# A state-space block and a gated mixture on one core: products of the first chunk moved to GpSimd, second scores ahead of the first outputs, and a carried state moved within the fourth step

## The chip, the cores and the metric

One core of a Trainium2 chip runs the whole kernel. The metric is device time in microseconds of one execution; the kernel before has a median of 639.62 us over four runs (639.5 to 639.63). TensorE is called PE, VectorE DVE, ScalarE ACT, GpSimd POOL and SyncE SP, as in the profile.

## The reference, cut to what matters

Two blocks follow one another. The first is a recurrent block (4 sequences, 8 heads, 768 tokens, head size 32, state size 16), worked in chunks; the second sends its output, seen as 3072 tokens of width 256, through four experts and adds them with normalised weights.

```python
# first block, for each chunk
cum = np.cumsum(la, axis=-1)                       # la = log(clip(a))
L = np.exp(cum[..., :, None] - cum[..., None, :]) * causal
M = np.einsum('bhin,bhjn->bhij', Cc, Bc) * L       # scores, masked by decays
y = M @ xc + (Cc @ state) * exp(cum)
state = decay_full * state + sum over the chunk of B x decay_from_j
# second block
p = domain_probs / (domain_probs.sum(-1, keepdims=True) + 1e-09)
for e in range(E):                                 # E = 4, F = 1024
    out += p[:, e:e + 1] * (np.maximum(x @ w1[e], 0) @ w2[e])
```

## The kernel before, in words

**Chunks.** The first block is worked in 24 chunks of 128 tokens of one sequence, all eight heads at once. The first four (numbers 0 to 3) are the beginnings of the four sequences, the next four continue them, and so on. For a chunk c these helpers exist:

- `spread(c)` (L331, PE) copies the decays a of chunks 0 to 2 to all partitions, into four PSUM banks; later chunks get them by a DMA, `load_decays` (L134, tile ab), from a DRAM copy acut_d that `store_decays(0)` writes from ScalarE's queue (L286). `store_decays(1)` does the same for ac_d, which `load_heads` reads (L146, tile ah).
- `decay_part(c, 0)` and `decay_part(c, 1)` (L364, DVE) are scans that make the decay matrices LT of the two halves of the heads. Part 1 ends with a GpSimd product that writes the decayed B into the last columns of MT (L369). `decay_part(c, 2)` is for chunks with an incoming state: a scan dec of ah (L347, DVE) and its product with C, cts (L350, POOL).
- `masks(c)` (L378, ACT) writes ctm, the rows of C of the even and the odd heads apart. `scores` (L393, PE) makes the scores g in four PSUM tiles of two heads each, numbered 0 to 3.
- `masked(cs, rs)` (L405, DVE) multiplies scores by LT into MT, one instruction for each number. `aside(c, q)` does one number in another way: ScalarE copies g to SBUF (gs, L412) and GpSimd multiplies (L413).
- `outputs` (L462, PE) and, for chunk 1, `outputs_apart` (L428) make y from MT; ScalarE copies it to yT (L471, L432) and the chunk's own state to A (L478, L435).
- `carry(c)` (L486 to L493, DVE) turns A into the state that the next chunk of that sequence receives: a transpose S and a product M with a mask.

**Steps.** The second block is worked in six blocks of 512 tokens (128 of each sequence, four chunks), each in eight steps n (four experts, two halves of an expert's width). From step 2 on, the products are arranged in seven where eight would be plain (fmul, L523, for the first layer; smul, L608, for the second), on sums of the weights that GpSimd makes (L189 to L193) and stores for later blocks (L201, L207). In a step, `snap` copies a PSUM bank (ACT, L530), `total` adds it to the other bank (DVE, L535, tile z), `gated` applies the maximum and the expert's weight (DVE, L545, tile h) and `diff` makes differences of gated tiles (DVE, L552, tile hT). The two PSUM banks of the first layer are X and Y; the steps that make chunk 4 and later use X and Y for two of the four score tiles as well.

**What sets the order.** The order is written out by hand: each engine gets its instructions in the order in which the Python code records them, and semaphores hold an instruction until its data and its buffer are ready. The first chunks are a written list at the end of the function (from `turn(1)` on). Then a loop over n records each step, and chunks 4 and later are spread over it: `scanned` chunks get their LT, `scored` chunks their masks, scores and masked products, `done` chunks their outputs. Work left from the step before is in the list `late`: two differences and, behind them, a `carry`. In the steps of the first block that score chunks (n = 3 and n = 6, where `behind` is true), the first two entries of `late` come behind the first gated tile, and the carry and `decay_part(c, 2)` behind `gated(n, "21", "X")`, directly in front of the scores:

```python
        gated(n, "21", "X")
        for work in late[2:] if behind else []:
            work()
        for c in scored if behind else []:
            decay_part(c, 2)
```

The ScalarE copies of `aside` and of `outputs` stand in one queue, so the order of the calls decides which is first.

Of the kernel before, what the change touches and what calls it, by code (L numbers as in the profile page):

```python
# [17 lines left out]
def kernel(  # L18
# [68 lines left out]
    att = ctx.enter_context(tc.tile_pool(name="att", bufs=2))  # L87
    ffn = ctx.enter_context(tc.tile_pool(name="ffn", bufs=2))
    ps_att = ctx.enter_context(tc.tile_pool(name="ps_att", bufs=2, space=bass.MemoryType.PSUM))
    ps_f = ctx.enter_context(tc.tile_pool(name="ps_f", bufs=1, space=bass.MemoryType.PSUM))  # L90
    ps_s = ctx.enter_context(tc.tile_pool(name="ps_s", bufs=1, space=bass.MemoryType.PSUM))
# [15 lines left out]
    def turned_round(c):  # L107


        return c >= CPB and c % 2 == 1  # L110
# [44 lines left out]
    def load_w1(n):  # L155
        e, jj = divmod(n % SPB, JJ)
        t1 = wt1[n] = wts.tile([P, 7, HB], FP32, tag="wt1", name="wt1", bufs=5)
        for k in range(2):
            w = 2 - 2 * k
            a_ = 2 if n < SPB or k else 1  # L160
            nc.sync.dma_start(
                out=t1[:, w:w + a_],
                in_=w1[e, k * P:k * P + P].rearrange("p (a f) -> p a f", a=2)[
                    :, 0:a_, jj * HB:jj * HB + HB])
        if n >= SPB:
            nc.sync.dma_start(out=t1[:, S3:], in_=w1_d[n % SPB])
# [117 lines left out]
    def store_decays(kind):  # L284
        d, sb = ((acut_d, a_cut), (ac_d, a_sb))[kind]
        nc.scalar.dma_start(  # L286
            out=d.rearrange("c h s -> (c h) s").rearrange("(p r) s -> p r s", r=2), in_=sb)
# [3 lines left out]
    def turn_gates(pool, tag):  # L291

        rows = T // P * E
        pp = pool.tile([rows, P], FP32, tag=tag, name="pp")
        nc.tensor.transpose(pp, pr.rearrange("p i e -> p (i e)"), ident[:, 0])
        p_sb = const.tile([rows, P], FP32, name="p_sb")
        gate["rows"] = p_sb
        nc.scalar.copy(out=p_sb, in_=pp)
# [24 lines left out]
    def spread(c, homes):  # L323


        s = st[c]
        s["a"] = []
        for q, (pool, tag) in enumerate(homes):
            k = slice(32 * q, 32 * q + 32)
            b = pool.tile([P, NT * P], FP32, tag=tag, name="a")  # L330
            nc.tensor.matmul(  # L331
                out=b, lhsT=one[k].to_broadcast([32, P]), rhs=a_q[k, c].rearrange("p t s -> p (t s)"),
                start=True, stop=True, tile_position=(32 * q, 0))
            s["a"].append(b)

    def decays(c):
        for part in range(3):
            decay_part(c, part)
# [34 lines left out]
    def masks(c):  # L373

        s = st[c]
        m = s["ctm"] = att.tile([HN, NT, P], FP32, tag="ctm", name="ctm")
        for t in range(NT):
            nc.scalar.mul(m[:, t], s["xb"][:, OCT:OCT + P], tmask[:, t:t + 1])  # L378

    def scores(cs, homes):  # L380

        for c in cs:
            st[c]["g"] = {}
        for r, (pool, tag) in enumerate(homes):
            g = pool.tile([P, len(cs), NT, P], FP32, tag=tag, name="g")
            for j, c in enumerate(cs):
                st[c]["g"][r ^ 2 * turned_round(c)] = g[:, j]
        for j, c in enumerate(cs):
            s = st[c]
            for r in range(NQ):  # L390
                k = slice(32 * r, 32 * r + 32)
                g = s["g"][r ^ 2 * turned_round(c)]
                nc.tensor.matmul(  # L393
                    out=g.rearrange("p t s -> p (t s)"), lhsT=s["xb"][k, OBT:OBT + P],
                    rhs=s["ctm"][k].rearrange("p t s -> p (t s)"),
                    start=(j == 0), stop=True, tile_position=(32 * r, 0),
                    skip_group_check=True)

    def masked(cs, rs):
        for r in rs:  # L400
            for c in cs:
                q = r ^ 2 * turned_round(c)
                h = slice(NT * q, NT * q + NT)
                s = st[c]
                nc.vector.tensor_mul(s["MT"][:, h, 0:P], s["g"][q], s["LT"][:, h])  # L405

    def aside(c, q):

        s = st[c]
        h = slice(NT * q, NT * q + NT)  # L410
        g = att.tile([P, NT, P], FP32, tag="gs", name="gs")
        nc.scalar.copy(out=g, in_=s["g"][q])  # L412
        nc.gpsimd.tensor_mul(s["MT"][:, h, 0:P], g, s["LT"][:, h])  # L413
# [322 lines left out]
    turn(1, 3)  # L736
    masks(0)
    scores([0], homes)
    store_decays(0)
    decays(0)  # L740
    aside(0, 3)
    masks(1)
    load_w1(1)
    load_tokens(3)
    load_decays(3)
    load_w2(0)
    spread(1, banks)
    masked([0], (2, 0, 1))
    turn_gates(ps_att, "att")
    outputs([0])  # L750
    scores([1], ((ps_f, "X"), (ps_s, "acc0"), (ps_s, "acc1"), (ps_att, "att")))
    decay_part(1, 0)
    aside(1, 0)
    decay_part(1, 1)
# [61 lines left out]
    late = []  # L816
    states = [2, 3]
    for n in range(PLAIN, NS):
        k, r = divmod(n, SPB)

        ahead = CPB * (k + 1)
        scanned = [ahead + d for d in {0: [0], 2: [1], 4: [2], 5: [3]}.get(r, [])]
        scored = [ahead + d for d in {3: [0, 1], 6: [2, 3]}.get(r, [])]
        done = [ahead + d for d in {4: [0, 1], 7: [2, 3]}.get(r, [])]
        if k == NBLK - 1:
            scanned, scored, done = [], [], []
        ending = r == 0 and k > 0
        e = r // JJ
        if r % JJ == 0 and n + JJ < NS:
            load_gate(*divmod(n // JJ + 1, E))  # L830
        if PLAIN + 2 < n + 2 < NS:
            load_w1(n + 2)
            load_w2(n + 2)
        opened(n)
        total(n, 1, "11")
        gated(n, "11", "z11")
        behind = scored and k == 0
        for work in late[:2] if behind else late:
            work()
        if r == 1 and k > 0:  # L840
            combine(k - 1, 0)
            combine(k - 1, 1)
        for c in scanned:
            decay_part(c, 0)
        for c in scored:
            masks(c)
        if k > 0 and 2 <= r < CPB + 2:
            leave(k - 1, r - 2)
        smul(n - 1, 1)
        fmul(n, 6)  # L850
        snap(n, 6)
        smul(n - 1, 3)
        if ending:
            keep(k - 1, 0)
        if done:
            outputs(done)
            states.extend(done)
        fmul(n, 5)
        fmul(n, 7)
        snap(n, 7)  # L860
        total(n, 7, "22")
        smul(n - 1, 7)
        smul(n - 1, 5)
        if ending:
            keep(k - 1, 1)
        gated(n, "22", "z22")
        if r == 1 and k > 0:
            combine(k - 1, 2)
        for c in scanned:
            decay_part(c, 1)  # L870
        for c in scored if not behind else []:
            decay_part(c, 2)
        if n == PLAIN:
            sum_w2(0, 1)
        elif n == SPB - 4:
            sum_w1(n + 2)
        elif n >= SPB - 3:
            sum_w2(n)
        if n < CPB:
            load_chunk(n + CPB)  # L880
        for c in scanned if n >= CPB else []:
            if c + 2 < NCH:
                load_decays(c + 2)
        for c in done:
            if c + CPB < NCH:
                load_tokens(c + CPB)
                load_heads(c + CPB)
        fmul(n, 3)
        total(n, 6, "12")
        fmul(n, 4)  # L890
        gated(n, "21", "X")
        for work in late[2:] if behind else []:
            work()
        for c in scored if behind else []:
            decay_part(c, 2)
        if not scored:
            gated(n, "12", "z12")
        if r == SPB - 1 and k < NBLK - 1:
            sums(k + 1)
        smul(n - 1, 6)  # L900
        if scored:
            scores(scored, ((ps_att, "att"), (ps_att, "att"), (ps_f, "Y"), (ps_f, "X")))
            masked(scored, (3, 2, 0, 1))
            gated(n, "12", "z12")
        smul(n - 1, 2)
        diff(n, "T3", "22", "12")
        smul(n - 1, 4)
        if n == PLAIN:
            sum_w2(1, 1)
        if n != SPB - 4:  # L910
            sum_w1(n + 2)
        if PLAIN < n < SPB - 4:
            sum_w2(n + 1)
        diff(n, "T1", "12", "11")
        if r == 1 and k > 0:
            turned_out(k - 1)
        late = [lambda n=n: diff(n, "T2", "22", "T1"), lambda n=n: diff(n, "T4", "21", "T2")]
        if states:
            late.append(lambda c=states.pop(0): carry(c))
# [48 lines left out]
```

## Time and profile before

| | |
|---|---|
| median of four runs | 639.62 us |
| the profiled execution | 638.56 us |
| its span, first to last instruction | 636.8 us |
| PE busy | 631.6 us (99%) |
| DVE busy | 484.6 us (76%) |
| ACT busy | 119.4 us (19%) |
| POOL busy | 113.2 us (18%) |
| granted PE clock, mean | 0.999 |
| second-layer products L608 in the chain that ended last | 43% of the span |
| first-layer products L523 in that chain | 44% (X 25%, Y 19%) |
| scores L393 and outputs L462 in that chain | 2% and 2% |
| masked products L405 and scans L364 in that chain | 1% and 1% |

The span is the time from the first to the last instruction of the profiled execution; 1.76 us of that execution's time lie outside it. The chain that ended last is followed back from the last instruction, at each step to what released it. A line of the timeline gives the start and the length in us, the engine, the line of the kernel, the operation, the tiles written and read, the shapes, the number of instructions taken together, and in brackets the idle time of the engine before it with what ended it. A line of the list of waits gives who waited for whom, the sum in us, how often, and the longest.

### The profile page before, as it was taken

The page shows a single profiled execution, that of the slowest core. Times are in us where ns is not written, and L with a number is a line of the kernel's source. Part 1 is how long each engine was busy: PE and PEld are TensorE (multiplying, and loading weights), DVE is VectorE, ACT ScalarE, POOL GpSimd, SP SyncE. Part 2 cuts the span into 40 slices and gives each one's busy share as a digit, 9 for nine tenths or more (in the row PEclk, how much of TensorE's full clock was granted, in tenths as well). Part 3 has the DMA queues.
Part 4 walks back from the last instruction along what each step waited for, and adds up shares of the span by engine and source line. Part 5 has one row for each costly group of instructions (what it writes and reads, how often), then busy time and mean ns, then how long its engine had stood idle before and what let it go on. Part 6 is the DMA issues. An engine that isn't in the chain of part 4 may idle for free.

```text
span 636.8 us, 9256 instructions
## 1 busy us (share of the span) xinstructions
PE 631.6 (99%) x3405; PEld 537.7 (84%) x3405; DVE 484.6 (76%) x811; ACT 119.4 (19%) x263; POOL 113.2 (18%) x163
## 2 busy tenths in 40 slices
PE   9999999999999999999999999999999999999997
PEld 5888788888888888888888888888888888888886
DVE  7869989887787788678687778778867677756555
ACT  4011221212111221122211221122111211111111
POOL 5786757020001002000002000000100000100001
PEclk9999999999999999999999999999999999999999
DMA  7798994755566392656384566639365643156001
GB/s 226 250 355 312 296 324 157 278 174 166 187 206 236 90 372 73 230 177 215 129 281 155 171 197 198 228 107 355 92 214 181 221 162 133 61 165 229 1 1 33
DMA packets 98512, 121.61 MB, mean 191 GB/s; under 512 B 29528, under 2 KB 81956, under 8 KB 98468
## 3 DMA queue, kind: packets, MB, share of 16 engines
q1 hardware_dynamic: 95512, 111.20, 52.8%
q0 software_dynamic: 2432, 9.50, 3.8%
q8 instruction: 27, 0.44, 0.3%
q10 hardware_dynamic: 524, 0.32, 0.2%
q14 instruction: 17, 0.14, 0.1%
HBM read 108.16 MB, written 12.83 MB: 190 GB/s over the span
## 4 chain that ended last, share of the span: by engine, by line
PE 96%; DVE 2%; issue 1%; POOL 0%; ACT 0%; POOLq 0%; DVEq 0%
PE acc L608 43%; PE X L523 25%; PE Y L523 19%; PE acc L589 2%; PE g L393 2%; PE y L462 2%; PE X L572 1%; PE Y L572 1%; PE y L450 1%; DVE MT L405 1%; DVE hT L552 1%; DVE LT L364 1%; PE t L729 1%; DVE h L545 0%; PE a L331 0%
## 5 line engine op out<-in xcount | busy, mean ns | idle before, releaser
L535 DVE TENSOR_TENSOR z<-Y,snap 128x512 f32<-128x512 f32 x138 | 94.6, 685 | 118.2 <-ACT snap L530 66.8
L608 PE MATMUL acc<-hT,wt 128*128 128x256 f32 x736 | 181.1, 379 | 0.0
L530 ACT COPY snap<-X 128x512 f32<-128x512 f32 x138 | 80.8, 586 | 464.9 <-PE X L523 396.5
L608 PEld LDWEIGHTS acc<-hT,wt 128*128 128x128 f32 x736 | 140.1, 190 | 18.8
L608 PE MATMUL acc<-h,wt 128*128 128x256 f32 x552 | 142.6, 381 | 0.0
L523 PE MATMUL X<-yS,wt 128*128 128x256 f32 x552 | 141.8, 379 | 0.0
L608 PEld LDWEIGHTS acc<-h,wt 128*128 128x128 f32 x552 | 104.2, 190 | 16.8 <-issue 2.0
L523 PEld LDWEIGHTS X<-yS,wt 128*128 128x128 f32 x552 | 105.0, 190 | 14.3 <-issue 0.3
L545 DVE SCALAR_TENSOR_TENSOR h<-z,gate 128x512 f32<-128x512 f32 x138 | 99.5, 721 | 3.5 <-PE acc L589 0.4
L523 PE MATMUL Y<-yT,wt 128*128 128x256 f32 x368 | 94.6, 380 | 0.5 <-DVE z L535 0.5
L523 PEld LDWEIGHTS Y<-yT,wt 128*128 128x128 f32 x368 | 68.9, 190 | 11.3 <-DVE z L535 0.9
L552 DVE TENSOR_TENSOR hT<-h,hT 128x512 f32<-128x512 f32 x92 | 66.1, 718 | 1.8
L552 DVE TENSOR_TENSOR hT<-h,h 128x512 f32<-128x512 f32 x92 | 65.0, 748 | 1.4
L364 DVE TENSOR_TENSOR_SCAN LT<-ab,ident 128x512 f32<-128x512 f32 x42 | 52.0, 1241 | 0.0
L523 PE MATMUL Y<-yS,wt 128*128 128x256 f32 x184 | 48.3, 385 | 0.0
L523 PE MATMUL X<-yT,wt 128*128 128x256 f32 x184 | 47.2, 379 | 0.0
L369 POOL TENSOR_TENSOR MT<-xb,LT 128x128 f32<-128x128 f32 x20 | 8.6, 428 | 204.1 <-PE Y L523 71.8
L405 DVE TENSOR_TENSOR MT<-g,LT 128x256 f32<-128x256 f32 x94 | 32.3, 413 | 10.5 <-PE g L393 10.4
L523 PEld LDWEIGHTS Y<-yS,wt 128*128 128x128 f32 x184 | 34.2, 190 | 6.4 <-issue 2.2
L523 PEld LDWEIGHTS X<-yT,wt 128*128 128x128 f32 x184 | 35.0, 190 | 4.7
L545 DVE SCALAR_TENSOR_TENSOR h<-X,gate 128x512 f32<-128x512 f32 x50 | 34.2, 683 | 5.2 <-PE X L523 3.6
L350 POOL TENSOR_TENSOR cts<-ctm,dec 128x256 f32<-128x256 f32 x20 | 14.1, 727 | 130.2 <-DVE dec L347 130.1
(103 smaller groups left out, 324.4 us busy)
## 6 DMA issues: line engine op xcount, KB each, us to landing
wt<-in_w_dram SPq DMA_DIRECT2D x112, 256.0 KB
wt<-w_d SPq DMA_DIRECT2D x40, 640.0 KB
wt<-w_d SPq DMA_DIRECT2D x40, 512.0 KB
ab<-acut_d SPq DMA_DIRECT2D x21, 512.0 KB
gate<-p_d SPq DMA_DIRECT2D x23, 256.0 KB
w_d<-wt POOLq DMA_DIRECT2D x8, 640.0 KB, 4.2
wt<-in_w_dram SPq DMA_DIRECT2D x40, 128.0 KB
w_d<-wt POOLq DMA_DIRECT2D x8, 512.0 KB, 6.9
```

Of the source, the lines that this page charges most:

```text
L350: nc.gpsimd.tensor_mul(cts, s["ctm"], dec.unsqueeze(1).to_broadcast([HN, NT, P]))
L364: nc.vector.tensor_tensor_scan(out=LT[:, i * w:i * w + w], data0=s["a"][i], data1=ident.rearrange("p h s -> p (h s)")[:, :w], initial=0.0, ...
L393: nc.tensor.matmul(out=g.rearrange("p t s -> p (t s)"), lhsT=s["xb"][k, OBT:OBT + P], rhs=s["ctm"][k].rearrange("p t s -> p (t s)"), start ...
L405: nc.vector.tensor_mul(s["MT"][:, h, 0:P], s["g"][q], s["LT"][:, h])
L462: nc.tensor.matmul(out=y[32 * q:32 * q + 32, t, 0:w], lhsT=s["xb"][:, h * D:h * D + D], rhs=s["MT"][:, NT * q + t, 0:w], start=(k == 0 and ...
L523: nc.tensor.matmul(out=f[bank][:, j], lhsT=wt1[n][:, w, j * P:j * P + P], rhs=rhs, start=(i in (1, 2, 5) and j == 0), stop=(j == JJ - 1), ...
L530: nc.scalar.copy(out=s, in_=first[n]["X"])
L535: nc.vector.tensor_add(z, first[n]["Y"], first[n][i])
L545: nc.vector.scalar_tensor_tensor(out=h, in0=first[n][src], scalar=0.0, in1=g.unsqueeze(1).to_broadcast([P, JJ, HB]), op0=ALU.max, op1=ALU. ...
L552: nc.vector.tensor_sub(h[o], h[x], h[y])
L572: nc.tensor.matmul(out=f[bank][:, j], lhsT=wt1[n][:, w, j * P:j * P + P], rhs=yT[k][:, i, cols], start=(i == 0 and j == 0), stop=(i == 1), ...
L608: nc.tensor.matmul(out=acc[k, u][:, half], lhsT=w2_op(n, w)[:, j], rhs=rhs[:, j], start=(begins and j == 0), stop=(n % SPB == SPB - 1 and ...
```

## The change

Two things are changed. In the written list, chunk 0 gets its scores 0 and 1 by way of ScalarE and GpSimd (two `aside`) and 2 and 3 on VectorE, where it had 3 by the first way and 2, 0 and 1 on VectorE; the two `aside` stand between the halves of the scans, so ahead of `masks(1)`, of the store of acut and of GpSimd's L369. And the scores of chunk 1 are recorded ahead of the outputs of chunk 0.

In the loop, at n = 3 (not at n = 6), the carry and `decay_part(c, 2)` of chunks 4 and 5 are recorded behind `gated(n, "22", "z22")`, so ahead of `total(n, 6, "12")` and `gated(n, "21", "X")` on VectorE.

```diff
     scores([0], homes)
+    decay_part(0, 0)
+    aside(0, 0)
+    aside(0, 1)
+    decay_part(0, 1)
+    masks(1)
     store_decays(0)
-    decays(0)
-    aside(0, 3)
-    masks(1)
     load_w1(1)
...
     spread(1, banks)
-    masked([0], (2, 0, 1))
+    masked([0], (2, 3))
     turn_gates(ps_att, "att")
+    scores([1], ((ps_f, "X"), (ps_s, "acc0"), (ps_s, "acc1"), (ps_att, "att")))
     outputs([0])
-    scores([1], ((ps_f, "X"), (ps_s, "acc0"), (ps_s, "acc1"), (ps_att, "att")))
     decay_part(1, 0)
...
         behind = scored and k == 0
+        last = behind and r == 6
...
             decay_part(c, 1)
-        for c in scored if not behind else []:
+        for work in late[2:] if behind and not last else []:
+            work()
+        for c in scored if not last else []:
             decay_part(c, 2)
...
         gated(n, "21", "X")
-        for work in late[2:] if behind else []:
+        for work in late[2:] if last else []:
             work()
-        for c in scored if behind else []:
+        for c in scored if last else []:
             decay_part(c, 2)
```

## The prediction

> **What bounds the kernel now.** I read the engine table and the list of what TensorE waited for first: they say how much a change can win. TensorE (PE) is busy 631.6 of 636.8 us, and over the whole span it waits for data only three times.
>
> ```profile
> PE 631.6 (99%) x3405; PEld 537.7 (84%) x3405; DVE 484.6 (76%) x811; ACT 119.4 (19%) x263; POOL 113.2 (18%) x163
> ```
> ```profile
> PE y L428 <- POOL MT L369: 0.5, 1, 0.5
> PE Y L523 <- DVE z L535: 0.5, 1, 0.5
> PE turned L655 <- DVE o L686: 0.3, 1, 0.3
> ```
>
> The third is at the end, which the change doesn't touch. The first two lie in the change's two places. From the first to the second PE is busy without a gap, and so it is from the second to the end. So the first product after the start (L428 at 11.31 us, followed by L331 at 12.30) is a clock for everything behind it, and the stall in front of 73.78 us is the only later place where time can be had. Next I read the timeline of both places (start us, length us, engine, line, operation).
>
> ```profile
> 7.05 1.06 DVE L405 TENSOR_TENSOR MT<-g,LT 128x256 f32<-128x256 f32 x3
> 8.02 2.42 DVE L364 TENSOR_TENSOR_SCAN LT<-a,ident 128x256 f32<-128x256 f32 x4
> 8.05 0.99 PE L462 MATMUL y<-MT,xb 128*32 128x144 f32 x16
> 8.98 0.71 PE L393 MATMUL g<-ctm,xb 32*128 32x256 f32 x8
> 9.08 0.37 ACT L471 COPY yT<-y 128x256 f32<-128x256 f32 x1 [0.66 <-PE y L462]
> 9.35 0.19 ACT L478 COPY A<-y 128x32 f32<-128x32 f32 x1
> 9.71 0.37 ACT L412 COPY gs<-g 128x256 f32<-128x256 f32 x1 [0.16 <-PE g L393]
> 10.16 0.72 POOL L413 TENSOR_TENSOR MT<-gs,LT 128x256 f32<-128x256 f32 x1 [1.84 <-ACT gs L412]
> 10.55 1.09 DVE L405 TENSOR_TENSOR MT<-g,LT 128x256 f32<-128x256 f32 x3
> 10.84 0.41 POOL L369 TENSOR_TENSOR MT<-xb,LT 128x128 f32<-128x128 f32 x1
> 11.31 1.07 PE L428 MATMUL y<-MT,xb 128*32 128x144 f32 x16 [0.53 <-POOL MT L369]
> ```
>
> The reader is to see two chains that meet in y(1), the outputs of the second chunk. One is ScalarE's copy gs, GpSimd's product L413, then L369 (ends 11.25). The other is VectorE's three products, which end at 11.64; the weight loads of y(1) pause 0.20 us for them after the first four. Both must get shorter for y(1) to end earlier.
>
> ```profile
> 58.91 0.69 DVE L535 TENSOR_TENSOR z<-Y,snap 128x512 f32<-128x512 f32 x1 [0.56 <-PE Y L523]
> 60.83 0.73 DVE L347 TENSOR_TENSOR_SCAN dec<-ah,zeros 128x128 f32<-128x128 f32 x2
> 61.40 1.41 POOL L350 TENSOR_TENSOR cts<-ctm,dec 128x256 f32<-128x256 f32 x2 [3.42 <-DVE dec L347]
> 61.74 2.74 DVE L405 TENSOR_TENSOR MT<-g,LT 128x256 f32<-128x256 f32 x8 [0.18 <-PE g L393]
> 65.11 2.23 DVE L552 TENSOR_TENSOR hT<-h,h 128x512 f32<-128x512 f32 x2
> 68.93 2.35 DVE L552 TENSOR_TENSOR hT<-h,hT 128x512 f32<-128x512 f32 x2
> 73.78 1.13 PE L523 MATMUL Y<-yT,wt 128*128 128x256 f32 x4 [0.51 <-DVE z L535]
> ```
>
> From 61.74 to 73.73 VectorE has no gap, and its end releases PE. But at 61.74 it had itself waited 0.18 us for the scores g, and before that 0.56 us for Y.
>
> **The change, step 1: the start.** VectorE loses one of the three products: 1.06/3 = 0.35 us, so the scans of chunk 1 (8.02) begin at 7.70 and end at 10.12, and its products end at 11.32 instead of 11.64.
>
> GpSimd gets two products of 0.72 us where it had one, now ahead of L369. ScalarE copies the first two scores instead of the fourth and does so before masks(1) and the store of acut. The first score is there by about 5.8 (L393 starts at 5.45), a copy takes 0.37 with the next 0.27 behind it: copies to 6.44, masks to 7.1. GpSimd is busy with a_cut until 6.23; its products run 6.28 to 7.8, L369 to 8.2. It ended at 8.31 before, so nothing waits for it.
>
> PE now does g(1) before y(0). The first product of g(1) writes into bank X, which the first scan of chunk 1 must have read: 7.70 + 0.62 = 8.32, so g(1) runs 8.37 to 9.02. Then y(0), 16 passes in 0.63 us without a pause (row L462 at 17.51 to L393 at 18.14): 9.00 to 9.70. It ended at 9.04 before, so ScalarE's yT is 0.64 us later. In ScalarE's queue gs(1) still stands behind yT and A, as the order of the built program shows. That g is ready earlier is therefore worth nothing: gs(1) starts at 9.72 + 0.27 + 0.19 = 10.18 instead of 9.71. L413 and L369 follow with the same distances, +0.47, and y(1) starts at 11.78 instead of 11.31. VectorE's products are done by then, so the 0.20 pause goes: 11.78 + 0.63 = 12.41 to the next matmul, against 12.30. **Step 1 costs +0.1 us.** The bounds: if y(1) waited for VectorE alone, −0.32; if its passes took as long as before (0.99), +0.47.
>
> Moved queues: the store of acut leaves at 7.1 instead of 6.26 (+0.8), and SP's load of ab(3), which waited for it to 10.71, leaves at about 11.5; w2(0), p_d and w2(1) stand behind it. The ab in front landed by 15.97 (SP's w2(2) waited 1.1 us for it), so it lands by 16.8 now, and its reader is the scan at 18.23. w2(0) is first read at 21.07. This costs nothing; without the cover each microsecond past 18.23 would be one on PE, as y(3) starts 0.6 us after its last product. The store of ac_d waits for a different DMA semaphore in the new program (that of acut, long done, instead of the one of p_d), so it can leave at 14.8 instead of 17.59, and SP's ah(4) before 23.48. Nobody waits for ah there: 0.
>
> **Step 2: carry(2) and the two dec scans at n = 3.** They take 60.38 to 61.56 now, 1.18 us. They move to 58.27, behind h22, into the idle 0.56 us. z12 then starts at 59.4 instead of 58.91, h21 at 60.1 instead of 59.77, ending at 60.8. The eight products can't start earlier than 61.74, since PE ends g at 61.7; VectorE's own gain is zero there, only more idle time. What is late next is bank X: h21 must be read out before the fourth score product, whose weights go in at about 60.8. I price that at 0 to +0.15, and take +0.05.
>
> The gain comes through GpSimd. cts waited for dec (3.42 us idle) and now starts 2.1 us earlier, at 59.3; the sums of w1(5) behind it run 60.7 to 63.9 instead of 62.78 to 66.79, mostly beside the products L405. Beside those a GpSimd sum takes 0.72 to 0.73 (62.78, 63.57) and they take 0.34 each, as in other rows: they don't hurt each other. Beside the differences they do: an alone hT takes 0.68, the pairs above 2.23 and 2.35 instead of 1.36, one h 1.02 instead of 0.69, one M 0.58 instead of 0.29. That is 0.87 + 0.99 + 0.33 + 0.29 = 2.48 us lost to six GpSimd sums, 0.41 each. With the first two gone from there, four remain (w2(4), from 64.8): 1.65. The chain gains 0.83, more than the 0.51 us of the stall, so the stall goes: **−0.47** with the +0.05 for bank X. More can't be had here, for PE is then bound by its own work. The low end is −0.51, the high end +0.15: no stall removed, and bank X late.
>
> A rule here speaks against the change. By the Trainium skill, "SBUF — State Buffer", Who interferes with whom, the port pair that VectorE and GpSimd share is locked for a whole instruction, and whoever comes second waits fully. The rows show 0.41 us per meeting, not the 0.73 of a whole GpSimd sum, because VectorE is sometimes the first. If it always came second, four meetings would cost 2.9 us, more than the 2.48 of now, the stall would stay and the time would be 639.7.
>
> **The sum.** +0.10 − 0.47 = −0.37 us. The profiled execution took 638.56 (span 636.8 and 1.76 around it), so it would be 638.2. The median of the runs shown is 639.62, 1.06 above it; the difference carries over: 639.62 − 0.37 = **639.25**. About 0.2%, 1.28 us, is what a measurement of this kernel can tell from no change.
>
> **The rivals.**
>
> *The stall stays (639.7).* w2(4) meets the same differences that w1(5) met, or carry(2) pushes bank X. Then only +0.1 remains. For it: GpSimd's work is not less, only earlier. Against it: two sums less in the stretch.
>
> *The start gains (638.8).* If y(1) follows VectorE's products (11.32), −0.32, and −0.47 at the stall. Against it: ScalarE's order; for it, only that the durations of copies might overlap more.
>
> *Slower: GpSimd's products are held by VectorE's scans (640.2).* The place is L413 of chunk 0, which now runs beside the scans of 4.70 to 7.14. One sum beside a scan took 1.62 (31.00, with a scan that reads ab from SBUF). Two of 1.62 and an L369 of 1.0 would end GpSimd at 10.5 instead of 8.2, but y(0) is not due before 9.0: it decides from 9.0 on, and costs 1:1 from there, +0.95 to +1.5 for ends of 9.95 to 10.5. Against it: L413 at 10.16 took 0.72 while a scan that reads a from PSUM ran to 10.44. Price: 639.25 + 0.95 = 640.2.
>
> *Late transfer (641 or more).* ab(3) lands after 18.23, 1.4 us later than I have it.
>
> **How the numbers follow.** Forecast 0.50, stall stays 0.22, start gains 0.12, GpSimd held 0.10, late transfer 0.06. The range 638.8 to 640.2 takes in the first three and the lower edge of the fourth. Slower by over 0.2% (above 640.9) are the late transfer and the far end of the held products: 0.08. Faster by over 0.2% (below 638.34) would need 1.28 us where both stalls together hold 1.04: 0.02. Within: 0.90.
>
> **What would show it.** Step 1 is right if g(1) starts near 8.4, y(0) near 9.0, gs(1) near 10.2 and y(1) near 11.8 with L331 at 12.4; wrong if y(1) starts before 11.5 or after 12.0. Step 2 is right if cts starts near 59.4, the eight products still near 61.8, the two pairs of differences take less in sum than 4.58, and the list of PE's waits has lost the line with z. The prediction is wrong if PE shows a wait that isn't in the list above: for MT of y(0), for ab, or for bank X.

## The result, and the profile after

The change makes the kernel faster: median 638.66 us of 34 runs (638.0 to 638.86) against 639.61 us of 52 runs (638.44 to 639.67). The ratio is 0.9986, interval 0.9981 to 0.999. That is 0.95 us, inside the 0.2% named in the prediction as "within", but 0.14 us below the lower end of the range, and 2.6 times the forecast gain of 0.37. The profiled execution took 638.10 us, its span is 636.3.

Executions of the same kernel differ among themselves (27 of the 52 runs of before lie at 639.61 to 639.67, the others are spread down to 638.44), and the first trace of before, 638.56, is of one of the shortest, so a second trace of each kernel is used below: e3 of the kernel before (639.64) and e4 of the changed one (638.69), both near the medians.

The list of PE's waits, of the first trace after:

```profile
PE y L428 <- POOL MT L369: 0.9, 1, 0.9
PE t L729 <- PEq L965: 0.8, 1, 0.8
PE g L393 <- ACT p_sb L298: 0.4, 1, 0.4
PE turned L655 <- DVE o L686: 0.3, 1, 0.3
```

The line with z in front of L523 is gone. The wait in front of y(1) has grown from 0.5 to 0.9, and one in front of the scores of chunk 1 is new; the wait at L729, at the very start, is as long as before. The start, in the timeline of the same trace (start us, length us, engine, line, operation):

```profile
7.05 0.73 DVE L405 TENSOR_TENSOR MT<-g,LT 128x256 f32<-128x256 f32 x2
8.48 0.71 PE L393 MATMUL g<-ctm,xb 32*128 32x256 f32 x8 [0.35 <-ACT p_sb L298]
9.12 0.70 PE L462 MATMUL y<-MT,xb 128*32 128x144 f32 x16
9.88 0.37 ACT L471 COPY yT<-y 128x256 f32<-128x256 f32 x1 [1.46 <-PE y L462]
10.22 1.08 DVE L405 TENSOR_TENSOR MT<-g,LT 128x256 f32<-128x256 f32 x3
10.23 0.39 ACT L412 COPY gs<-g 128x256 f32<-128x256 f32 x1
11.38 0.41 POOL L369 TENSOR_TENSOR MT<-xb,LT 128x128 f32<-128x128 f32 x1
11.85 0.70 PE L428 MATMUL y<-MT,xb 128*32 128x144 f32 x16 [0.95 <-POOL MT L369]
12.48 0.31 PEld L331 LDWEIGHTS a<-a_q,const-float32-1.0 32*128 32x128 f32 x8 [0.23 <-issue]
```

The reader is to see that VectorE's products are ready at 11.30, 0.34 us sooner than before, and that nobody profits: gs(1) starts 0.52 us later than before (9.71), behind yT, and y(1) 0.54 later. Because the pause inside y(1) is gone, only 0.18 us are left at L331 (12.30 before). In the second pair of traces, e3 and e4, it is 0.16:

```profile
12.90 0.31 PEld L331 LDWEIGHTS a<-a_q,const-float32-1.0 32*128 32x128 f32 x8 [0.23 <-issue]
13.06 0.31 PEld L331 LDWEIGHTS a<-a_q,const-float32-1.0 32*128 32x128 f32 x8 [0.23 <-issue]
```

The profile puts the new wait of the scores g down to ScalarE's copy p_sb, which ends at 8.42, just ahead of them. By the code they wait for the first scan of chunk 1, which reads bank X; e10 below decides for the scan.

Now steps 3 and 4 of the first trace after:

```profile
58.89 0.73 DVE L347 TENSOR_TENSOR_SCAN dec<-ah,zeros 128x128 f32<-128x128 f32 x2
59.47 1.41 POOL L350 TENSOR_TENSOR cts<-ctm,dec 128x256 f32<-128x256 f32 x2 [1.32 <-DVE dec L347]
60.70 1.28 PE L393 MATMUL g<-ctm,xb 32*128 32x256 f32 x16
62.02 2.74 DVE L405 TENSOR_TENSOR MT<-g,LT 128x256 f32<-128x256 f32 x8 [1.22 <-PE g L393]
64.68 1.38 DVE L545 SCALAR_TENSOR_TENSOR h<-z,gate 128x512 f32<-128x512 f32 x1
66.09 2.23 DVE L552 TENSOR_TENSOR hT<-h,h 128x512 f32<-128x512 f32 x2
69.57 1.41 DVE L552 TENSOR_TENSOR hT<-h,hT 128x512 f32<-128x512 f32 x2
```

cts starts 1.9 us sooner than before. VectorE's eight products start no sooner; they wait 1.22 us for the scores instead of 0.18. But the second pair of differences takes 1.41 us instead of 2.35, and with it the stall is gone. How large the stall was is told by the weight loads of PE, not by its matmuls. Here are three answers of the timeline for them: the first trace before, the second trace before (e3), and the second trace after (e4).

```profile
71.17 1.70 PEld L608 LDWEIGHTS acc<-hT,wt 128*128 128x128 f32 x8
73.78 0.73 PEld L523 LDWEIGHTS Y<-yT,wt 128*128 128x128 f32 x4 [0.91 <-DVE z L535]
```
```profile
71.76 1.70 PEld L608 LDWEIGHTS acc<-hT,wt 128*128 128x128 f32 x8
74.85 0.73 PEld L523 LDWEIGHTS Y<-yT,wt 128*128 128x128 f32 x4 [1.39 <-DVE z L535]
75.61 0.41 PEld L523 LDWEIGHTS X<-yS,wt 128*128 128x128 f32 x2
```
```profile
72.07 1.70 PEld L608 LDWEIGHTS acc<-hT,wt 128*128 128x128 f32 x8
73.85 0.79 PEld L523 LDWEIGHTS Y<-yT,wt 128*128 128x128 f32 x4
74.66 0.84 PEld L523 LDWEIGHTS X<-yS,wt 128*128 128x128 f32 x4
```

The eight matmul instructions of the second layer take 1.73 us in the chain of work, so the next weights were due at 72.90, 73.49 and 73.80. They came 0.88, 1.36 and 0.05 us late. The matmul rows at the same places give 0.51 and 0.99 us of idle time, for the end of a matmul is modelled in these profiles, and here reaches 0.40 us past the point at which the weights went idle.

A part of the lateness comes back: the next group of weights (its row of e3 holds two of the four, since that answer ends at 76 us) follows 0.76 us behind the late one, against 0.81 in e4. From the start of the eight to that next group it is 3.85 us in e3 and 2.59 in e4. So the stall is worth 1.26 us there, and 0.78 in the first pair of traces (74.54 − 71.17 before, 2.59 again after).

The scores g of step 3 are the other place in the loop, first in e3 and then in e4, each with the group behind them:

```profile
61.12 0.74 PEld L393 LDWEIGHTS g<-ctm,xb 32*128 32x128 f32 x16 [0.33 <-issue]
62.20 0.73 PEld L608 LDWEIGHTS acc<-h,wt 128*128 128x128 f32 x4 [0.33 <-issue]
```
```profile
61.29 0.88 PEld L393 LDWEIGHTS g<-ctm,xb 32*128 32x128 f32 x16 [0.33 <-issue]
62.50 0.73 PEld L608 LDWEIGHTS acc<-h,wt 128*128 128x128 f32 x4 [0.33 <-issue]
```

They take 1.08 us before and 1.21 after. From e3 to e4 the sum is +0.16 at the start, +0.13 at these scores and −1.26 at the stall, −0.97; the last copy starts at 634.85 and 633.89, −0.96. The medians differ by 0.95.

### The profile page after: what moved, and what is told of

It is laid out like the page before. It is cut to its first block, busy times and chain, and to the rows that moved or that the text cites. A ratio compares the mean times of both kernels' runs of the same rounds, so it can differ in the third digit from the quotient of the medians.

```text
span 636.3 us, 9258 instructions
## 1 busy us (share of the span) xinstructions
PE 630.9 (99%) x3405; PEld 537.6 (84%) x3405; DVE 483.2 (76%) x810; ACT 119.6 (19%) x264; POOL 112.8 (18%) x164
## 4 chain that ended last, share of the span: by engine, by line
PE 98%; issue 1%; DVE 0%; POOL 0%; ACT 0%; POOLq 0%
PE acc L608 44%; PE X L523 25%; PE Y L523 19%; PE acc L589 2%; PE y L462 2%; PE g L393 2%; PE X L572 1%; PE Y L572 1%; PE y L450 1%; PE t L729 1%; DVE LT L364 0%; PE a L331 0%; POOL MT L413 0%; POOL MT L369 0%; PE y L428 0%
## 5 line engine op out<-in xcount | busy, mean ns | idle before, releaser
L523 PE MATMUL X<-yS,wt 128*128 128x256 f32 x552 | 141.8, 379 | 0.0
L523 PEld LDWEIGHTS X<-yS,wt 128*128 128x128 f32 x552 | 105.0, 190 | 14.3 <-issue 0.3
L523 PE MATMUL Y<-yT,wt 128*128 128x256 f32 x368 | 94.4, 379 | 0.0
L523 PEld LDWEIGHTS Y<-yT,wt 128*128 128x128 f32 x368 | 68.9, 190 | 10.5
L523 PE MATMUL Y<-yS,wt 128*128 128x256 f32 x184 | 48.3, 385 | 0.0
L523 PE MATMUL X<-yT,wt 128*128 128x256 f32 x184 | 47.2, 379 | 0.0
L369 POOL TENSOR_TENSOR MT<-xb,LT 128x128 f32<-128x128 f32 x20 | 8.6, 428 | 204.9 <-DVE LT L364 74.9
L405 DVE TENSOR_TENSOR MT<-g,LT 128x256 f32<-128x256 f32 x93 | 32.0, 414 | 11.5 <-PE g L393 11.4
L523 PEld LDWEIGHTS Y<-yS,wt 128*128 128x128 f32 x184 | 34.2, 190 | 6.4 <-issue 2.2
L523 PEld LDWEIGHTS X<-yT,wt 128*128 128x128 f32 x184 | 35.0, 190 | 4.7
```

What stands on the lines that cost most here:

```text
L523: nc.tensor.matmul(out=f[bank][:, j], lhsT=wt1[n][:, w, j * P:j * P + P], rhs=rhs, start=(i in (1, 2, 5) and j == 0), stop=(j == JJ - 1), ...
```

## The experiments

Theory P held that the start gains in the more frequent executions; theory Q, that the start always costs its 0.17 and that the stall is worth more than the first trace shows. Later, theory G held that the stall is made by GpSimd's sums meeting VectorE's operations on two SBUF tiles; theory V, that VectorE gains by having the carry and the scans out of the way.

**e1_start_only**: the first-chunk edits alone, the loop as before (the first three pieces of the diff).

> The edits of the first two chunks alone; the loop over the steps is as before. Theory P (the start depends on when TensorE gets its full clock, and the profiled executions, 638.56 and 638.10, are both ones of an early full clock): the start costs 0.17 us in an execution with an early full clock, as the two traces show (L331 at 12.48 instead of 12.30), but gains 0.3 to 0.5 in the more frequent executions with a late one, so the median goes from 639.61 to about 639.2. Theory Q (the start always costs what the profiled execution shows, and the step n = 3 gains more than the trace shows): median 639.8, 0.17 above before.

Measured: 639.79 us against 639.58, ratio 1.0004 (0.9995 to 1.0013). Eight of its 11 runs lie at 639.79 to 639.89, and 10 of the 21 of before at 639.61 to 639.62, the highest of them. So the cost is about 0.2 us, as Q has it, though the interval alone would allow none. L331 comes at 13.16 in its trace, of 639.89, 0.10 later than in e4: y(0) waits for L369 there and starts at 9.80 (9.71 in e4), which neither trace of the changed kernel shows. The gain of the start that P foretold isn't there.

**e2_n3_only**: the edit of the loop alone, the start as before.

> The edit of step n = 3 alone; the start is as before. Theory P: the weight loads of TensorE show a gap of 0.88 us in front of 73.78 in the trace before (they would have gone on at 71.17 + 1.73 = 72.90), which goes, while bank X costs 0.14 and about 0.05 of the wait stays: 0.69 to 0.75 us gained, median 638.9. Theory Q: the whole difference of the medians and the 0.17 of the start, 1.1 us: 638.5. The recorded forecast had 0.47 here: 639.15.

Measured: 638.51 against 639.58, ratio 0.9984 (0.9975 to 0.9993): 1.07 us gained, Q's number. P's price of the stall, 0.88, was that of one execution; 1.26 − 0.13 from e3 and e4 is 1.13.

**e3_before_again and e4_after_again**: both kernels once more, unchanged.

> The kernel before once more, for a second trace of it. Theory P: if its time is near 639.6 and not 638.6, TensorE's products of the first 8 us take longer than in the first trace, and L331 of the third chunk starts about 1 us later than 12.30, with the stall in front of L523 in step 4 as large as in the first trace. Theory Q: the start is as in the first trace (12.30) and the 1 us lies in step 3 or 4.

> The changed kernel once more, for a second trace of it. Theory P: if its time is near 638.7 and not 638.1, L331 of the third chunk starts about 0.6 us later than 12.48, and nothing else differs. Theory Q: no difference at the start; the 0.6 us lies elsewhere.

Measured: 639.64 and 638.69. Each theory was partly right. L331 starts 0.60 us later than in the first trace before (P: about 1), and 0.58 later after (P: 0.6). But the stall of before differs too, by 0.48: weights 1.36 us late and not 0.88. The two traces of before differ by 0.60 + 0.48 = 1.08 us, those of the changed kernel by the 0.58 alone, and so the medians are further apart than the first two traces. VectorE and GpSimd in the second trace before, where the meeting begins:

```profile
64.99 1.25 DVE L545 SCALAR_TENSOR_TENSOR h<-z,gate 128x512 f32<-128x512 f32 x1
66.28 2.76 DVE L552 TENSOR_TENSOR hT<-h,h 128x512 f32<-128x512 f32 x2
70.29 2.35 DVE L552 TENSOR_TENSOR hT<-h,hT 128x512 f32<-128x512 f32 x2
```
```profile
64.97 0.73 POOL L191 TENSOR_TENSOR wt<-wt 128x256 f32<-128x256 f32 x1
65.66 1.17 POOL L193 TENSOR_TENSOR wt<-wt 128x256 f32<-128x256 f32 x1
```

In this trace the sum L191 takes 0.73 us, as when it is alone, and h takes 1.25 instead of 0.69. In the first trace it was the other way: L191 took 1.28, h 0.68. The two instructions start 0.01 to 0.02 us apart in both. From there to the stall VectorE loses 0.56 + 1.40 + 0.99 = 2.95 us in this trace, 2.48 in the first. The traces of e1, e9 and e10, which have the loop of before, show the order of this one (h 1.25 or 1.26, weights idle for 1.38 to 1.40 us); the cheaper order stands in the first trace alone. That this first meeting decides the later ones is argued, not shown.

**e5_sums_ahead**: the kernel before, with GpSimd's four sums of w1(5) in front of cts.

```diff
+        if n == PLAIN + 1:
+            sum_w1(n + 2)
         for c in scored if behind else []:
             decay_part(c, 2)
...
-        if n != SPB - 4:
+        if n not in (SPB - 4, PLAIN + 1):
             sum_w1(n + 2)
```

> The kernel before, with one thing moved: at n = 3 GpSimd makes the sums of w1(5) ahead of cts (recorded in front of decay_part(c, 2)) and not behind it; VectorE's order is that of before. Theory G (the stall in front of L523 in step 4 is made by meetings of GpSimd's sums with VectorE's operations on two SBUF tiles): the sums run in the 3.4 us in which GpSimd waited for dec, the stall of 1.36 us goes without any cost at bank X, and the time is 638.2 to 638.4. Theory V (the gain comes from VectorE having the carry and the dec scans out of the way): VectorE's order is unchanged, so 639.6.

Measured: 638.38 against 639.63, ratio 0.9981 (0.9972 to 0.999). No instruction of VectorE was moved, and 1.25 us are gained, what the stall of e3 is worth. G holds, V falls. The sums now meet VectorE earlier, where it has time:

```profile
58.26 1.64 DVE L545 SCALAR_TENSOR_TENSOR h<-z,gate 128x512 f32<-128x512 f32 x1
61.25 0.87 DVE L493 TENSOR_TENSOR M<-S,qmask 128x128 f32<-128x128 f32 x1
62.69 2.71 DVE L405 TENSOR_TENSOR MT<-g,LT 128x256 f32<-128x256 f32 x8
69.83 1.41 DVE L552 TENSOR_TENSOR hT<-h,hT 128x512 f32<-128x512 f32 x2
```

The h at 58.26 takes 1.64 us instead of 0.69 and M 0.87 instead of 0.29, and the products start 0.36 later than in e3; the stall is gone all the same.

**e6_carry_only**: the kernel before, with only the carry moved behind h22 (made by `gated(n, "22", "z22")`) at n = 3.

```diff
+        for work in late[2:] if behind and r == 3 else []:
+            work()
         for c in scored if not behind else []:
             decay_part(c, 2)
...
-        for work in late[2:] if behind else []:
+        for work in late[2:] if behind and r == 6 else []:
             work()
```

> The kernel before, with only the carry (0.45 us of VectorE) moved behind h22 at n = 3; the dec scans stay in front of the scores. Theory G: dec and so cts and the sums come 0.45 us earlier, which takes at most one of six meetings of 0.41 to 0.56 us away: 639.1 to 639.6. Theory V: 0.45 of the 1.18 us moved, so the same share of the gain of 1.1, 0.42: 639.2.

Measured: 639.18 against 639.63, ratio 0.9993 (0.9984 to 1.0002), an interval that just takes in no change. Both theories gave this number, so by itself it doesn't tell them apart. The trace (of 638.94) shows VectorE's products waiting 0.63 us for g, so VectorE's own time was not what counted, and a shorter stall:

```profile
74.17 0.73 PEld L523 LDWEIGHTS Y<-yT,wt 128*128 128x128 f32 x4 [0.93 <-DVE z L535]
```

The weight loads idle for 0.93 us where they idle for 1.39 in e3. The pairs of differences take 2.76 and 2.35 us as in e3; the difference is h, which takes 0.79 and not 1.25, since L191 starts 0.49 us ahead of it here. So the loss is smaller by 1.25 − 0.79 = 0.46 us, just as much as the stall (1.39 − 0.93), as G has it.

**e7_dec_only**: the kernel before, with only the dec scans moved.

```diff
-        for c in scored if not behind else []:
+        for c in scored if not behind or r == 3 else []:
             decay_part(c, 2)
...
-        for c in scored if behind else []:
+        for c in scored if behind and r == 6 else []:
             decay_part(c, 2)
```

> The kernel before, with only the two dec scans (0.73 us) moved behind h22 at n = 3; the carry stays. Theory G: cts starts as early as in the change or 0.45 us earlier, the whole stall of 1.36 goes, and since h21 ends 0.4 us earlier than in the change, bank X is free in time and its 0.14 us is not paid: 638.3 to 638.4, below the 638.51 of both moved. Theory V: 0.73 of 1.18, so 0.68 gained: 638.9.

Measured: 638.37 against 639.63, ratio 0.998 (0.9971 to 0.9988). V would have 638.9. Half of the loop's change does better than the whole (638.51 in e2): the scores g and the group behind them start at 61.12 and 62.20 as in e3, 1.08 us apart, and h21, which must be read out of bank X first, at 60.37 as in e3 (60.71 in e4). So the 0.13 goes with the later h21.

**e8_gs_first**: the changed kernel, with gs(1) in front of yT.

```diff
-    outputs([0])
     decay_part(1, 0)
     aside(1, 0)
+    outputs([0])
```

> The changed kernel, with the first scan of chunk 1 and the aside of its first scores recorded ahead of the outputs of chunk 0, so that ScalarE's copy gs(1) stands in front of yT and A. If ScalarE's order is what makes y(1) late (start 11.85 in the first trace after), gs(1) starts near 9.1 instead of 10.23, L369 follows the last scan and ends near 10.7, and y(1) is then bound by VectorE's products, which end near 11.3: L331 at about 11.95 instead of 12.48, so 638.66 - 0.5 = 638.15. If y(1) is held by VectorE or by the outputs of chunk 0 anyway, no difference: 638.66.

Measured: 638.25 against 639.63, ratio 0.9979 (0.997 to 0.9988); 0.41 below the median of the changed kernel. The order of ScalarE's queue was the cost. The trace, whose first passes of L331 take 1.24 us as in e3 and e4:

```profile
9.82 0.37 ACT L412 COPY gs<-g 128x256 f32<-128x256 f32 x1 [0.81 <-PE g L393]
10.47 0.37 ACT L471 COPY yT<-y 128x256 f32<-128x256 f32 x1 [0.28 <-PE y L462]
11.95 0.39 PEld L428 LDWEIGHTS y<-MT,xb 128*32 128x32 f32 x12 [0.20 <-DVE MT L405]
12.57 0.31 PEld L331 LDWEIGHTS a<-a_q,const-float32-1.0 32*128 32x128 f32 x8 [0.23 <-issue]
```

y(1) pauses for VectorE's products again, as in before, and L331 comes at 12.57, 0.49 sooner than in e4 and 0.33 sooner than in e3.

**e9_aside_only** and **e10_scores_ahead_only**: the kernel before with one of the two edits of the start.

> The kernel before, with only the products of chunk 0 divided anew (two on GpSimd, two on VectorE); outputs of chunk 0 stay ahead of the scores of chunk 1, and the loop is as before. If the cost of the start comes from the scores being ahead of the outputs: y(0) waits only for GpSimd's L369 (8.43 in the first trace after, against 8.31), gs(1) stays near 9.7 and y(1) follows VectorE's products, which are 0.32 us earlier: 0.2 to 0.3 gained, 639.35. If the cost comes from the division itself: 639.8, as with both.

> The kernel before, with only the scores of chunk 1 recorded ahead of the outputs of chunk 0; products and loop are as before. If the order is the cost: the scores wait for the first scan of chunk 1, which ends at 8.71, so g runs from 8.75, y(0) to 10.1, gs(1) starts at 10.5 instead of 9.71, and y(1) at about 12.15 instead of 11.31, less the 0.2 us pause: L331 at 12.8 instead of 12.30, 640.1. If the division is the cost: 639.6.

Measured: e9 639.79 against 639.64, ratio 1.0006 (0.9996 to 1.0016), with wide runs (638.86 to 642.59); e10 640.14, ratio 1.0008 (0.9999 to 1.0017). Both intervals take in no change. But all 11 runs of e10 lie above all 23 of before (639.71 and up against 639.67 and down); for e9 the trace has to decide. e10 is as expected if the order is the cost, with L331 at 13.39 instead of 12.90:

```profile
9.37 0.34 PEld L393 LDWEIGHTS g<-ctm,xb 32*128 32x128 f32 x8 [0.85 <-ACT p_sb L298]
13.39 0.31 PEld L331 LDWEIGHTS a<-a_q,const-float32-1.0 32*128 32x128 f32 x8 [0.23 <-issue]
```

Here p_sb ends at 9.01, the same as in e4, while the scans of chunk 1 begin at 8.61 instead of 8.29, and the weights of g come 0.33 later (9.37 instead of 9.04). So it is the scan that holds the scores, and not p_sb, which the profile names. e9 contradicts the other half: the division gains nothing either. In its trace y(0) waits 0.6 us for L369, which GpSimd begins behind both products:

```profile
7.49 1.41 POOL L413 TENSOR_TENSOR MT<-gs,LT 128x256 f32<-128x256 f32 x2 [1.20 <-ACT gs L412]
8.86 0.42 POOL L369 TENSOR_TENSOR MT<-xb,LT 128x128 f32<-128x128 f32 x1
9.33 0.40 PEld L462 LDWEIGHTS y<-MT,xb 128*32 128x32 f32 x16 [0.80 <-POOL MT L369]
12.97 0.31 PEld L331 LDWEIGHTS a<-a_q,const-float32-1.0 32*128 32x128 f32 x8 [0.23 <-issue]
```

So the two edits belong together: with the scores ahead, y(0) is late anyway and hides the two products; with one product fewer, the first scan of chunk 1 ends about 0.33 us sooner and the scores can go. Together they cost 0.16 at L331 (e4), e9 alone 0.07, e10 alone 0.49, each against e3.

**e11_gs_first_dec_only**: the start of e8 and the loop of e7.

> The start of the run before last with gs(1) ahead of yT, and at n = 3 only the dec scans moved: the two best parts together. If they add: 639.62 - 0.33 at the start - 1.25 at the stall = 638.05. If the stall is moved by what the start does to the phase of the engines: up to 638.3.

Measured: 637.98 against 639.64 (8 runs), ratio 0.9976 (0.9966 to 0.9986). The two gains add (expected 638.05). It beats the kernel before by 1.66 us and the changed one, by the medians, by 0.68.

## Why the prediction was right or wrong, point by point

- *Step 1 costs +0.1 us.* Right in mechanism, 0.16 to 0.18 in size. The path was as told: GpSimd not late for y(0), the scores released by the first scan of chunk 1 (PE's weights at 8.44 instead of 8.37), gs(1) behind yT and A (10.23 against 10.18), y(1) at 11.85 against 11.78, L331 at 12.48 against 12.41. Two errors nearly cancel in gs(1): yT came 0.16 later than reckoned (9.88), and gs started 0.08 behind the start of A and not 0.19. The new wait in front of the scores is one for bank X, which the prediction's last paragraph calls a sign of being wrong; its own times for g(1) contain it. e8 shows ScalarE's order to be the cause of the late y(1).
- *The moved queues cost nothing.* Right: LT of chunk 3 had no wait, and PE has none there. The way was another: the store of acut left at 6.30 and not 7.1, while ScalarE's copies ran (6.19 to 6.83). That ab left at 11.14, near the forecast 11.5, is luck: from the store to ab it was 4.84 us, where it was 4.45 before. The first reader of w2(0), L589, starts at 23.07 and not at 21.07, which leaves more room.
- *Bank X, 0 to +0.15, taken as +0.05.* It is 0.13 to 0.14, the upper end; e7 pays nothing of it. (0.51 less 0.05 is 0.46, not the 0.47 of the prediction.)
- *The stall goes: −0.47.* **This is the step that failed**, in its size: the stall was worth not 0.51 us but 0.78 in the profiled execution and 1.26 in e3, and less the cost at bank X the loop gained 1.07 by the medians (e2). The mechanism was right: cts and the sums of w1(5) come earlier, run beside the products L405 and cost nothing there, and the meetings fall. The forecast loss of the changed kernel, 1.65 us, is 1.61 in e4 (h 0.69, the pairs 0.87 and 0.05), though not as 0.41 for each of four. But the stall was taken as 0.51 from the matmul's row, where the weight loads show 0.88; and it was taken from one execution; the four other traces with the loop of before (e1, e3, e9, e10) show weight loads idle for 1.38 to 1.40 where it showed 0.91. The bound "more can't be had here" came from the same row, and so did the figure of 1.04 for both stalls.
- *The difference carries over from the profiled execution to the median.* Wrong: the two traces first at hand differ by 0.46, the medians by 0.95, because in that execution of before GpSimd and VectorE met in a cheaper order, worth 0.48 us.
- *The rule on the shared port.* By the Trainium skill, "SBUF — State Buffer", Who interferes with whom, whoever comes second waits for the whole instruction. e3 agrees, by the start times of the rows, where VectorE is second: h takes 1.25 instead of 0.69. The first trace after doesn't: h starts at 64.68, 0.08 ahead of the sum L189, and still h takes 1.38 and the sum 0.74. The row of h begins while the product in front of it runs (to 64.76), so at such distances the rows don't tell who was first. That the stall would stay, as the prediction drew from it for the worst case, was not so. The same section says that a VectorE instruction with at most one SBUF input doesn't contend, outside the modes in which it uses both ports: the eight products L405 of step 3, with g in PSUM, take 2.71 to 2.74 us in all 13 traces, with cts and the sums at different places beside them.
- *The rivals.* The stall didn't stay, the start didn't gain, GpSimd's products were not held (0.71 us each beside scans), and no transfer was late (ab had landed by 16.62, its reader starts at 18.41).

## What to carry to other kernels

An engine that is off the critical path can set it through its meetings with another: here four sums on GpSimd that ran earlier, where VectorE reads PSUM or has time to wait, were worth the whole gain of the loop, and it is had without moving any instruction of VectorE (e5). The length of a stall of TensorE is read from its weight loads and from the pace of the products around it, and in more than one trace where a race of two engines decides it. In an in-order queue, an operand that is ready earlier is worth nothing until its instruction also stands earlier (e8).

## What the runs showed of the hardware

Executions of the same code differ in their first 6 us. In the two traces of before the first eight passes of L331 take 0.71 and 1.24 us, and the two of L729 behind them 0.92 and 1.18:

```profile
3.96 0.71 PE L331 MATMUL a<-a_q,const-float32-1.0 32*128 32x256 f32 x8
4.61 0.92 PE L729 MATMUL t<-const-float32-1.0 128*128 128x384 f32 x2
```
```profile
4.03 1.24 PE L331 MATMUL a<-a_q,const-float32-1.0 32*128 32x256 f32 x8
5.20 1.18 PE L729 MATMUL t<-const-float32-1.0 128*128 128x384 f32 x2
12.90 0.71 PE L331 MATMUL a<-a_q,const-float32-1.0 32*128 32x256 f32 x8
```

From there to L331 of chunk 2 the second execution is 0.60 us behind, and the changed kernel shows the same (0.58). The values between occur too: the eight passes take 0.71 in three of the 13 traces, 0.99 in e6, 1.18 in e11 and 1.23 or 1.24 in the other eight. In e3 the same eight passes take 1.24 us at 4.03 and 0.71 at 12.90, so it looks as if TensorE reached its full pace later in such an execution; the granted clock is recorded as 1.00 in both stretches, so no run here proves that. Whether the order in which L191 and h meet, at 0.01 to 0.02 us between them, turns with it stays open as well: the cheaper order was seen in one trace only.
